# Fewer, wider groups of query tiles in an attention stage, and moved weight scans behind it

## The chip, the cores and the metric

The program runs on one core of a Trainium2 chip. The metric is the device time of one execution in microseconds (us). Engines: PE = TensorE (PEld its weight loads), DVE = VectorE, ACT = ScalarE, POOL = GpSimd, SP = SyncE, whose queue issues the transfers.

## What is computed

A masked attention (4 batches, 8 heads, 576 positions, head size 64) and two feed-forward layers on its 2304 x 512 output:

```python
scores = q @ k.T / 8                       # heads 0-3: keys 0..31 back; heads 4-7: keys with the same index mod 32
x = softmax(where(mask, scores)) @ v       # reshaped to 2304 x 512
x = (h * cos(h)) @ w_out,  h = x @ w_in    # 512 -> 2048 -> 512
y = (silu(x @ w_gate) * (x @ w_val)) @ w_out2   # 512 -> 1536 -> 512
```

The weights arrive as 64-bit floats and are turned into float32 on the chip, then each into two float16 parts (high and low). The factor before the split comes from the largest absolute value of the whole matrix, so a matrix is scanned once before any of it can be split.

## The kernel before

**Attention.** Heads go in pairs; a unit is one pair in one batch, and there are 16 units, local ("l", keys up to 31 back) and strided ("s") in turn. A local unit has 9 tiles of 64 queries against 96 keys, a strided one 11 tiles of 54 queries against 54 keys. `groups` (L78) cuts a unit into groups: 3+3+3 tiles, or 4+4+3, so 48 groups in all, one for each step of the loop over `k` (L818). Groups of an s and an l unit alternate: a round of six steps does two units.

A group passes through the engines over eight steps (`LAGS`, L51). PE: `scores` (fp32 products L470, a filler of bfloat16 ones into the rest of the PSUM bank L472, and the mask added through an identity L473). DVE: `top` (row maximum, L478). One step later ACT: `exps` (one instruction per tile, L484). Two steps later DVE: `sums` (L493, L496), POOL: `norm` (L498). Five steps later PE: `transposes` (L504, L508) into one of two PSUM tiles `tp`, ACT: `evac` to SBUF (L515). Six: PE `values` (L526). Seven: ACT `put` (L539 local, L548 strided) into `xy`. After the last group the pipeline drains, with `keep_warm` (L816) and the first product of slot 0 on PE.

Other work is mixed in from a queue `fill`: `pump` (called in L858) emits entries until their cost passes a share per step, `PUMP` from step `KP` on. For w_in an entry chain converts a tile (ACT L254, DVE L257, L261, L265), and after the last tile, the scale and the split follow: high part on ACT (L275, entry cost 0), low part on DVE (L278, cost 0.7). Behind each low part stood one scan of a w_out tile (L204, cost 0.63). Raw tiles come through a ring of `RAW` = 6 buffers of 512 KB; `RELEASE` is the step from which those of w_out may start.

**First layer.** Its loop counts slots: 5 blocks of tokens times 16 columns tiles of w_in. A slot is one first product on PE (L584 to L586, 12 products of up to 512 columns), then ACT L617, DVE L620, ACT L624, DVE L627, ACT L631, POOL L632. Slot 0 lies in the drain. The first `HEAD` slots have only first products; from then on the queue of finished tiles is shortened to `MINLAG` at `RATE` a slot, each shortening being a second product with a w_out tile (`need(("out", m))`). In the same stretch the w_out tiles are converted and split ("cv", "arena") and w_gate and w_val scanned. `HSHARE`, `SHARE` and `SHARE2` set how much of `fill` a slot takes. The second layer follows once all its weights are rewritten.

Of the kernel before, what the change touches and what calls it, by code (L numbers as in the profile page):

```python
# [10 lines left out]
F32 = mybir.dt.float32  # L11
# [39 lines left out]
LAGS = (2, 5, 6, 7)  # L51
WARM = 11
PUMP, KP = 1.05, 8
XSAT = 12
EARLY, K0 = 1, 1
HEAD, HSHARE = 16, 0.8
RATE, MINLAG = 0.7, 2
ALONE = 4
RAW = 6
RELEASE = 30  # L60
# [3 lines left out]
SHARE, SHARE2, SB = 0.89, 0.82, 2  # L64
# [13 lines left out]
def groups(p):  # L78
    return [(0, 3), (3, 3), (6, 3)] if is_local(p) else [(0, 4), (4, 4), (8, 3)]


def build(tc, qk_l, qk_s, v_l, v_s, w_in, w_out, w_gate, w_val, w_out2, fixed, out):
    nc = tc.nc
    wide = w_in.dtype != F32
    with ExitStack() as ctx:
# [322 lines left out]
        words = [128, 2 * LW, 2 * SW]  # L408
        fix = ap.tile([128, sum(words)], F32, name="fix", bufs=1)
        id32, ml, ms = (fix[:, sum(words[:i]):sum(words[:i + 1])] for i in range(3))  # L410
        ml, ms = (t.bitcast(BF16).rearrange("p (n w) -> p n w", n=4) for t in (ml, ms))
        e_s = [ap.tile([128, 2, 64, 2], F32, name=f"e_s{i}", bufs=1) for i in range(4)]
        e_l = [ap.tile([128, 3, LW + 1], F32, name=f"e_l{i}", bufs=1) for i in range(4)]
# [38 lines left out]
        class Group:  # L452
# [7 lines left out]
            def scores(self):  # L460
# [3 lines left out]
                mask = (ml[:, 0:3] if self.g == 0 else ml[:, 1:4]) if self.loc else ms[:, 0:n]  # L464
# [35 lines left out]
            def transposes(self):  # L500
                if self.loc:
                    self.tp = pa.tile([128, self.n, 128], F32, name="tp")[0:LW]
                    for i in range(self.n):
                        nc.tensor.transpose(self.tp[:, i, :], self.t[:, i, 0:LW], id32)  # L504
                else:
                    self.tp = pa.tile([128, 2, 128], F32, name="tp")
                    for i in range(2):
                        nc.tensor.transpose(self.tp[:, i, :], self.t[:, i].rearrange("p k u -> p (k u)"), id32)  # L508

            def evac(self):  # L510
                if self.loc:
                    self.pt = ap.tile([LW, 3, 128], F32, name="pt", bufs=2)
# [860 lines left out]
```

## Time and profile before

| | us |
|---|---|
| runs | 862.55 median of 3 (862.11 to 862.92) |
| profiled execution | 862.11, span of its instructions 860.2 |
| PE / DVE / ACT / POOL busy | 845.0 / 653.6 / 520.5 / 196.5 |
| attention, to the first product of slot 1 | 102.05 |

The profile draws a matmul with a modelled end, so that its duration includes the run through the array, and neighbours overlap; what a phase takes from PE is read from its start to the next phase's start. ACT and DVE rows overlap in the same way. In the timeline, an fp32 product counts as two instructions.

### The profile page before, as it was taken

Reading aid. Unit: us, or ns where it says so; the run is one execution under the profiler, and the core shown is the slowest. Engines: PE = TensorE matmul, PEld = TensorE weight load, DVE = VectorE, ACT = ScalarE, POOL = GpSimd, SP = SyncE. Lnnn points to the kernel's source line nnn. Section 1 sums busy time; section 2 is a strip of 40 time slices with the busy share of each in tenths; the row PEclk is TensorE's granted clock in tenths of the full one; section 3 lists DMA queues with packets and bytes.
Section 4 is the critical chain, followed back from the end, with each engine's and each line's share of the span. In section 5 each row is a group of like instructions: output and inputs, shape, how many; then the busy total and the mean of one; then the engine's idle time right before and its main releaser. Section 6 shows DMA issues by size and latency. Waiting matters only on the chain.

```text
span 860.2 us, 18371 instructions
## 1 busy us (share of the span) xinstructions
PE 845.0 (98%) x7223; PEld 601.9 (70%) x7223; DVE 653.6 (76%) x1256; ACT 520.5 (61%) x1047; POOL 196.5 (23%) x249
## 2 busy tenths in 40 slices
PE   9999999999999999999999999999999999999998
PEld 5776544444444444555666787888888899999998
DVE  6999989997888978789996378567656755665562
ACT  6898889654657767768885466545344444444440
POOL 4444234211446446422223000000000000000000
PEclk9999999999999999999999999999999999999999
DMA  9998832896567566415356157667776777788894
GB/s 366 408 370 269 278 102 74 288 340 252 164 205 248 190 209 206 174 49 175 118 210 239 73 186 274 219 224 258 231 273 224 257 266 276 291 302 315 320 331 150
DMA packets 53606, 202.23 MB, mean 235 GB/s; under 512 B 5264, under 2 KB 15888, under 8 KB 49680
## 3 DMA queue, kind: packets, MB, share of 16 engines
q1 hardware_dynamic: 53520, 201.06, 66.9%
q8 instruction: 57, 0.93, 0.4%
q14 instruction: 29, 0.24, 0.1%
HBM read 177.05 MB, written 23.99 MB: 234 GB/s over the span
## 4 chain that ended last, share of the span: by engine, by line
PE 82%; DVE 10%; ACT 5%; issue 2%; DMA 1%; POOL 0%; ACTq 0%; DVEq 0%
PE acc L737 14%; PE bank L584 13%; PE bank L586 13%; PE bank L585 13%; PE acc L584 9%; PE acc L586 9%; PE acc L585 9%; DMA raw<-w_in 1%; DVE xs L278 1%; PE bank L470 1%; DVE arena L710 1%; DVE ls L493 1%; DVE arena L1235 1%; DVE tb L620 1%; ACT xy L548 1%
## 5 line engine op out<-in xcount | busy, mean ns | idle before, releaser
L584 PE MATMUL bank<-xs,wi 128*128 128x256 f16 (+3 forms) x776 | 231.1, 298 | 5.2 <-DVE arena L1235 2.3
L586 PE MATMUL bank<-xs,wi 128*128 128x256 f16 (+3 forms) x776 | 231.1, 298 | 0.0
L585 PE MATMUL bank<-xs,wi 128*128 128x256 f16 (+3 forms) x776 | 231.1, 298 | 0.0
L632 POOL TENSOR_TENSOR arena<-tb,arena 128x512 f16<-128x512 f32 (+1 forms) x80 | 91.2, 1141 | 239.1 <-ACT arena L631 223.8
L585 PEld LDWEIGHTS <-wi 128*128 128x128 f16 x880 | 86.1, 98 | 42.7 <-issue 8.6
L584 PE MATMUL acc<-arena 128*128 128x512 f16 (+1 forms) x320 | 114.5, 358 | 0.0
L585 PE MATMUL acc<-arena 128*128 128x512 f16 (+1 forms) x320 | 114.5, 358 | 0.0
L586 PE MATMUL acc<-arena 128*128 128x512 f16 (+1 forms) x320 | 114.5, 358 | 0.0
L584 PEld LDWEIGHTS <-wi 128*128 128x128 f16 x880 | 86.1, 98 | 36.0 <-issue 1.1
L586 PEld LDWEIGHTS <-wi 128*128 128x128 f16 x880 | 86.1, 98 | 34.8
L737 PEld LDWEIGHTS <-arena 128*128 128x128 f16 x1080 | 100.7, 98 | 8.2
L722 POOL TENSOR_TENSOR wi<-tb 128x256 f32<-128x256 f32 (+1 forms) x30 | 20.2, 673 | 340.5 <-DVE tb L704 340.5
L704 DVE SCALAR_TENSOR_TENSOR tb<-tb,c,arena 128x512 f32<-128x512 f32 (+1 forms) x60 | 41.6, 693 | 61.3 <-ACT tb L699 61.3
L707 ACT ACTIVATE arena<-tb 128x256 f16<-128x256 f32 (+3 forms) x59 | 28.9, 489 | 94.3 <-DVE tb L704 90.5
L585 PEld LDWEIGHTS <-arena 128*128 128x128 f16 x600 | 58.7, 98 | 34.1 <-issue 1.4
L737 PE MATMUL acc<-arena 128*128 128x256 f16 (+1 forms) x702 | 82.0, 265 | 0.0
L586 PEld LDWEIGHTS <-arena 128*128 128x128 f16 x600 | 58.7, 98 | 32.9
L584 PEld LDWEIGHTS <-arena 128*128 128x128 f16 x600 | 58.7, 98 | 32.6
L631 ACT ACTIVATE arena<-tb 128x512 f16<-128x512 f32 (+1 forms) x80 | 46.7, 583 | 53.0 <-PE acc L586 51.4
L617 ACT ACTIVATE tb<-bank,quarter,c 128x512 int32<-128x512 f32 (+1 forms) x74 | 53.7, 726 | 34.2 <-PE bank L586 26.4
L1235 DVE TENSOR_TENSOR arena<-bank,cv 128x512 f32<-128x512 f32 (+1 forms) x60 | 38.1, 636 | 45.1 <-PE bank L586 44.1
L699 ACT ACTIVATE tb<-arena,c 128x512 f32<-128x512 f32 (+1 forms) x60 | 40.8, 679 | 40.4 <-DVE arena L1235 39.4
(144 smaller groups left out, 1728.7 us busy)
## 6 DMA issues: line engine op xcount, KB each, us to landing
wi<-w SPq DMA_DIRECT2D x20, 1792.0 KB, 8.1
arena<-w SPq DMA_DIRECT2D x60, 576.0 KB, 4.8
raw<-w_out SPq DMA_DIRECT2D x56, 512.0 KB, 4.7
arena<-w SPq DMA_DIRECT2D x10, 1792.0 KB, 8.9
raw<-w_gate SPq DMA_DIRECT2D x24, 512.0 KB, 4.0
raw<-w_val SPq DMA_DIRECT2D x24, 512.0 KB, 5.7
w<-arena SPq DMA_DIRECT2D x42, 256.0 KB, 3.2
raw<-w_in SPq DMA_DIRECT2D x16, 512.0 KB, 9.1
```

The costliest lines, as they stand in the source:

```text
L584: nc.tensor.matmul(out=o, lhsT=w[:, 0, c], rhs=x[0], start=first, stop=False, **kw)
L585: nc.tensor.matmul(out=o, lhsT=w[:, 0, c], rhs=x[1], start=False, stop=False, **kw)
L586: nc.tensor.matmul(out=o, lhsT=w[:, 1, c], rhs=x[0], start=False, stop=last, **kw)
L617: nc.scalar.activation(out=c["w"].bitcast(I32), in_=c["ph"], func=AF.Identity, scale=turn[c["blk"]], bias=quarter)
L631: nc.scalar.activation(out=g[:, 0, 0:n], in_=w, func=AF.Copy)
L632: nc.gpsimd.tensor_tensor(out=g[:, 1, 0:n], in0=w, in1=g[:, 0, 0:n], op=ALU.subtract)
L699: nc.scalar.activation(out=t, in_=gate, func=AF.Silu, scale=turn_g[c["blk"]])
L704: nc.vector.scalar_tensor_tensor(out=t, in0=t, scalar=s_g[c["blk"]], in1=c["C"][m][:, 1, 0:c["n"]], op0=ALU.mult, op1=ALU.mult)
L707: nc.scalar.activation(out=to, in_=src, func=AF.Copy, scale=2.0 ** -11)
L722: nc.gpsimd.tensor_tensor(out=t_sums[:, 0, 0:h], in0=c["t"][0][:, h:2 * h], in1=c["t"][0][:, 0:h], op=ALU.subtract)
L737: nc.tensor.matmul(out=o[:, c], lhsT=w[:, 256 * i + 128 * c:256 * i + 128 * c + 128], rhs=unit(u)[:, x:x + h], start=j == c == i == 0, sto ...
L1235: nc.vector.tensor_tensor(out=c["C"][m][:, :, h * right:h * right + h], in0=p, in1=t, op=ALU.add)
```

## The change

A unit's tiles go in two groups: 5+4 local, 6+5 strided, so 32 groups and 39 steps instead of 48 and 56, a round being four steps. Fillers and tiles take the new widths; a local group of five is transposed into both `tp` tiles. Three buffers for exponentials instead of four, lags one step shorter. The w_out scans leave the places behind the low parts and stand behind all of them. `PUMP` goes to 1.4 from step 6, the second products start in slot 19 at 1.3 a slot, and the shares of a slot rise slightly. V tiles are loaded at a round's start for that round. Not shown: mask widths, the tile shapes of `mx`, `ls`, `pt`, and the host's layout of the masks.

```diff
--- before.py
+++ after.py
@@ -48,20 +48,21 @@
-LAGS = (2, 5, 6, 7)
+LAGS = (2, 4, 5, 6)
+ROUND = 4
 WARM = 11
-PUMP, KP = 1.05, 8
+PUMP, KP = 1.4, 6
 XSAT = 12
 EARLY, K0 = 1, 1
-HEAD, HSHARE = 16, 0.8
-RATE, MINLAG = 0.7, 2
+HEAD, HSHARE = 19, 0.8
+RATE, MINLAG = 1.3, 2
...
-RELEASE = 30
+RELEASE = 25
...
-SHARE, SHARE2, SB = 0.89, 0.82, 2
+SHARE, SHARE2, SB = 0.92,0.85,2
...
@@ -76,7 +77,7 @@
 def groups(p):
-    return [(0, 3), (3, 3), (6, 3)] if is_local(p) else [(0, 4), (4, 4), (8, 3)]
+    return [(0, 5), (5, 4)] if is_local(p) else [(0, 6), (6, 5)]
@@ -405,12 +406,12 @@
-        e_s = [ap.tile([128, 2, 64, 2], F32, name=f"e_s{i}", bufs=1) for i in range(4)]
-        e_l = [ap.tile([128, 3, LW + 1], F32, name=f"e_l{i}", bufs=1) for i in range(4)]
+        e_s = [ap.tile([128, 3, 64, 2], F32, name=f"e_s{i}", bufs=1) for i in range(3)]
+        e_l = [ap.tile([128, 5, LW + 1], F32, name=f"e_l{i}", bufs=1) for i in range(3)]
...
@@ -469,25 +470,25 @@
-                nc.tensor.matmul(out=b[:, 288:512], lhsT=ones16, rhs=hot[:, 0:224], start=False, stop=False)
+                nc.tensor.matmul(out=b[:, n * w:512], lhsT=ones16, rhs=hot[:, 0:512 - n * w], start=False, stop=False)
                 nc.tensor.matmul(out=self.sc, lhsT=id16, rhs=mask, start=False, stop=True)
...
             def exps(self):
-                self.t = (e_l if self.loc else e_s)[(self.i // 2 * 3 + self.g) % 4]
+                self.t = (e_l if self.loc else e_s)[(self.i // 2 * 2 + self.g) % 3]
...
@@ -498,21 +499,21 @@
             def transposes(self):
-                if self.loc:
-                    self.tp = pa.tile([128, self.n, 128], F32, name="tp")[0:LW]
-                    for i in range(self.n):
-                        nc.tensor.transpose(self.tp[:, i, :], self.t[:, i, 0:LW], id32)
-                else:
-                    self.tp = pa.tile([128, 2, 128], F32, name="tp")
-                    for i in range(2):
-                        nc.tensor.transpose(self.tp[:, i, :], self.t[:, i].rearrange("p k u -> p (k u)"), id32)
+                self.tp = []
+                for a, z in ((0, 3), (3, 5)) if self.loc and self.n > 4 else ((0, self.n if self.loc else 3),):
+                    t = pa.tile([128, 4, 128], F32, name="tp")[0:LW if self.loc else 128, 0:z - a]
+                    self.tp.append((a, z, t))
+                    for i in range(a, z):
+                        nc.tensor.transpose(t[:, i - a, :], self.t[:, i, 0:LW] if self.loc
+                                            else self.t[:, i].rearrange("p k u -> p (k u)"), id32)
             def evac(self):
...
-                nc.scalar.activation(out=self.pt, in_=self.tp, func=AF.Copy)
+                for a, z, t in self.tp:
+                    nc.scalar.activation(out=self.pt[:, a:z], in_=t, func=AF.Copy)
...
@@ -803,22 +804,25 @@
         top_later("in")
-        scan_later("out", 0)
+        later(1.0, lambda: None)
         scale_later(TW_IN, "in")
-        split_chain([("in", j, wi) for j in range(M1)], 2, lambda j: scan_later("out", j + 1) if j + 1 < M1 else top_later("out"))
+        split_chain([("in", j, wi) for j in range(M1)], 2)
+        for j in range(M1):
+            scan_later("out", j)
+        top_later("out")
...
         def keep_warm():
-            t = bank()[:, 0:4 * LW].rearrange("p (n w) -> p n w", w=LW)
+            t = bank()[:, 0:5 * LW].rearrange("p (n w) -> p n w", w=LW)
...
-            i, g = 2 * (k // 6), k % 6
+            i, g = 2 * (k // ROUND), k % ROUND
...
-                if g in (3, 4) and i + g - 1 < len(units):
-                    scale_q(i + g - 1)
+                if g in (1, 2) and i + g + 1 < len(units):
+                    scale_q(i + g + 1)
...
-            if group(0) and g == 5:
-                for j in (i + 2, i + 3):
-                    if i and j < len(units):
+            if g == 0 and i >= 4:
+                for j in (i, i + 1):
+                    if j < len(units):
                         load_v(j)
+            if group(0) and g == ROUND - 1:
                 for j in (i + 6, i + 7):
                     if j < len(units):
                         load_qk(j)
```

**PE in the attention, before** (one s and one l group; `po` is the output of `values`, `fix` holds the mask):

```order
L470 MATMUL bank<-qks 64x54 x8
L472 LDWEIGHTS ones_77
L472 MATMUL bank<-hot,ones_77 128x224
L473 LDWEIGHTS id_76
L473 MATMUL bank<-fix,id_76 128x216
L526 MATMUL po<-pts,v_pair_109 64x54 x8
L508 MATMUL tp<-fix,e_s_99 128x128 x2
L470 MATMUL bank<-qkl 64x96 x6
L472 LDWEIGHTS ones_77
L472 MATMUL bank<-hot,ones_77 128x224
L473 LDWEIGHTS id_76
L473 MATMUL bank<-fix,id_76 128x288
```

**PE there, after:**

```order
L471 MATMUL bank<-qks 64x54 x12
L473 LDWEIGHTS ones_77
L473 MATMUL bank<-hot,ones_77 128x188
L474 LDWEIGHTS id_76
L474 MATMUL bank<-fix,id_76 128x324
L527 MATMUL po<-pt,vl 64x64 x8
L507 MATMUL tp<-fix,e_l_102 96x128 x5
L471 MATMUL bank<-qkl 64x96 x10
L473 LDWEIGHTS ones_77
L473 MATMUL bank<-hot,ones_77 128x32
L474 LDWEIGHTS id_76
L474 MATMUL bank<-fix,id_76 128x480
```

The products of a phase grew from 6 or 8 to 8 to 12, the filler shrank from 224 columns to 188 and 32, and the pieces come in 16 such pairs instead of 24.

**ACT in the drain, before,** up to the last `put` (L539; `wi` is the split of w_in):

```order
L548 ACTIVATE xy_69<-po 128x12x6
L548 ACTIVATE xy_70<-po 128x12x12
L515 ACTIVATE pts<-tp 128x256
L539 ACTIVATE xy_70<-po 128x192
L515 ACTIVATE pt<-tp 96x384
L275 ACTIVATE wi<-wi,s_1656 128x512
L548 ACTIVATE xy_69<-po 128x8x6
L548 ACTIVATE xy_70<-po 128x8x12
L275 ACTIVATE wi<-wi,s_1656 128x512
L539 ACTIVATE xy_70<-po 128x192
```

**ACT there, after** (its lines are one higher):

```order
L516 ACTIVATE pts<-tp 128x384
L276 ACTIVATE wi<-wi,s_1621 128x512 x2
L540 ACTIVATE xy_69<-po 128x192
L540 ACTIVATE xy_70<-po 128x128
L516 ACTIVATE pt<-tp 96x512
L276 ACTIVATE wi<-wi,s_1621 128x512 x2
L549 ACTIVATE xy_69<-po 128x14x6
L549 ACTIVATE xy_70<-po 128x14x12
L276 ACTIVATE wi<-wi,s_1621 128x512 x2
L540 ACTIVATE xy_70<-po 128x256
```

Between the last `exps` and the last `put`, five high parts stood before, and ten stand now, always two in a row.

**DVE in the drain, before:**

```order
L204 TENSOR_REDUCE pw_out<-raw 128x1
L496 RECIPROCAL ls<-ls 128x4
L493 TENSOR_REDUCE ls<-e_l_105 128x3
L151 TENSOR_SCALAR c_1967<-inv_1220,inv_1657 128x1
L278 SCALAR_TENSOR_TENSOR wi<-wi,s_1656 128x512
L496 RECIPROCAL ls<-ls 128x3
L204 TENSOR_REDUCE pw_out<-raw 128x1
L278 SCALAR_TENSOR_TENSOR wi<-wi,s_1656 128x512
```

**DVE there, after:**

```order
L279 SCALAR_TENSOR_TENSOR wi<-wi,s_1621 128x512 x2
L497 RECIPROCAL ls<-ls 128x6
L494 TENSOR_REDUCE ls<-e_l_101 128x4
L152 TENSOR_SCALAR c_1719<-inv_1209,inv_1622 128x1
L279 SCALAR_TENSOR_TENSOR wi<-wi,s_1621 128x512 x2
L497 RECIPROCAL ls<-ls 128x4
L279 SCALAR_TENSOR_TENSOR wi<-wi,s_1621 128x512 x9
L205 TENSOR_REDUCE pw_out<-raw 128x1
L621 SCALAR_TENSOR_TENSOR tb<-bank,c_1719,tb 128x512
L205 TENSOR_REDUCE pw_out<-raw 128x1 x2
```

Beside each low part stood one scan of w_out; now all the low parts come first, and the 16 scans lie between the first layer's own instructions.

## Rows read from the trace of the kernel before

**Rows 1.** The page, busy time of the engines.

```profile
PE 845.0 (98%) x7223; PEld 601.9 (70%) x7223; DVE 653.6 (76%) x1256; ACT 520.5 (61%) x1047; POOL 196.5 (23%) x249
```

**Rows 2.** Windows: busy us of each engine (instructions), granted clock, DMA share, GB/s.

```profile
40.00:50.00 10.00, 10.00 (x169) 7.23 (x168) 9.90 (x26) 9.76 (x40) 5.05 (x8) 1.00 1.03 410
...
180.00:190.00 10.00, 10.00 (x48) 4.51 (x47) 9.93 (x18) 4.63 (x8) 1.16 (x1) 1.00 0.98 361
```

**Rows 3.** Timeline of PE, one s and one l group: start, duration, instruction.

```profile
62.10 0.67 PE L470 MATMUL bank<-qks 64*64 64x54 f32 x16
62.71 0.27 PE L472 MATMUL bank<-hot,ones 128*128 128x224 bf16 x1
62.81 0.26 PE L473 MATMUL bank<-fix,id 128*128 128x216 bf16 x1
63.00 0.68 PE L526 MATMUL po<-pts,v_pair 108*64 108x54 f32 x16
63.61 0.44 PE L508 MATMUL tp<-fix,e_s 128*128 128x128 f32 x2
63.98 0.71 PE L470 MATMUL bank<-qkl 64*64 64x96 f32 x12
64.62 0.27 PE L472 MATMUL bank<-hot,ones 128*128 128x224 bf16 x1
64.73 0.29 PE L473 MATMUL bank<-fix,id 128*128 128x288 bf16 x1
64.94 0.57 PE L526 MATMUL po<-pt,vl 96*64 96x64 f32 x12
65.44 0.53 PE L504 MATMUL tp<-fix,e_l 128*96 128x128 f32 x3
65.91 0.50 PE L470 MATMUL bank<-qks 64*64 64x54 f32 x10
```

**Rows 4.** The same view, an s group of three tiles.

```profile
20.68 0.56 PE L470 MATMUL bank<-qks 64*64 64x54 f32 x12
21.16 0.27 PE L472 MATMUL bank<-hot,ones 128*128 128x224 bf16 x1
21.27 0.23 PE L473 MATMUL bank<-fix,id 128*128 128x162 bf16 x1
21.43 0.56 PE L526 MATMUL po<-pts,v_pair 108*64 108x54 f32 x12
21.92 0.44 PE L508 MATMUL tp<-fix,e_s 128*128 128x128 f32 x2
```

**Rows 5.** Timeline of ACT, from the last scores to the last `put`.

```profile
92.34 0.88 ACT L275 ACTIVATE wi<-wi,s 128x512 f16<-128x512 f32 x1
92.95 0.48 ACT L539 ACTIVATE xy<-po 128x192 f32<-128x192 f32 x1
93.17 0.65 ACT L515 ACTIVATE pt<-tp 96x384 f32<-96x384 f32 x1
93.53 0.96 ACT L484 ACTIVATE e_l<-bank,mx 128x96 f32<-128x96 f32 x3
94.21 0.90 ACT L275 ACTIVATE wi<-wi,s 128x512 f16<-128x512 f32 x1
...
101.65 0.35 ACT L539 ACTIVATE xy<-po 128x192 f32<-128x192 f32 x1
```

**Rows 6.** Timeline of PE: first product of slot 1, and its wait before the second products.

```profile
102.05 0.38 PE L584 MATMUL acc<-xs,wi 128*128 128x512 f16 x1 [0.50 <-ACT xy L539]
...
142.26 0.38 PE L584 MATMUL bank<-xs,wi 128*128 128x512 f16 x1 [1.08 <-DVE tb L627]
```

**Rows 7.** DVE groups by line from 102.1 to 142 us: busy us, mean ns.

```profile
L620 DVE SCALAR_TENSOR_TENSOR tb<-bank,c,tb 128x512 f32<-128x512 f32 x8 | 5.9, 743 | 0.3 <-ACT tb L617 0.3
L627 DVE SCALAR_TENSOR_TENSOR tb<-tb,bank 128x512 f32<-128x512 f32 x7 | 4.7, 678 | 1.0 <-ACT tb L624 1.0
...
L278 DVE SCALAR_TENSOR_TENSOR wi<-wi,s 128x512 f16<-128x512 f32 x5 | 3.7, 744 | 0.0
L204 DVE TENSOR_REDUCE pw_out<-raw 128x1 f32<-128x512 f32 x5 | 3.4, 680 | 0.0
```

More of the change, by code (lines that the diff above doesn't have):

```diff
@@ L407, in build @@
         pa = attn.enter_context(tc.tile_pool(name="pa", bufs=2, space=bass.MemoryType.PSUM))
-        words = [128, 2 * LW, 2 * SW]
+        words = [128, 5 * LW // 2, SW]
         fix = ap.tile([128, sum(words)], F32, name="fix", bufs=1)
         id32, ml, ms = (fix[:, sum(words[:i]):sum(words[:i + 1])] for i in range(3))
-        ml, ms = (t.bitcast(BF16).rearrange("p (n w) -> p n w", n=4) for t in (ml, ms))
-        e_s = [ap.tile([128, 2, 64, 2], F32, name=f"e_s{i}", bufs=1) for i in range(4)]
-        e_l = [ap.tile([128, 3, LW + 1], F32, name=f"e_l{i}", bufs=1) for i in range(4)]
+        ml, ms = (t.bitcast(BF16).rearrange("p (n w) -> p n w", n=n) for t, n in ((ml, 5), (ms, 2)))
+        e_s = [ap.tile([128, 3, 64, 2], F32, name=f"e_s{i}", bufs=1) for i in range(3)]
+        e_l = [ap.tile([128, 5, LW + 1], F32, name=f"e_l{i}", bufs=1) for i in range(3)]
         hot = ap.tile([128, 512], BF16, name="hot", bufs=1)
@@ L463, in scores @@
                 self.sc = b[:, 0:n * w].rearrange("p (n w) -> p n w", w=w)
-                mask = (ml[:, 0:3] if self.g == 0 else ml[:, 1:4]) if self.loc else ms[:, 0:n]
+                mask = ml[:, 1 if self.g else 0:][:, 0:n] if self.loc else ms[:, 0:1].to_broadcast([128, n, w])
                 for i in range(n):
@@ L471, in scores @@
                                          start=i == 0, stop=False)
-                nc.tensor.matmul(out=b[:, 288:512], lhsT=ones16, rhs=hot[:, 0:224], start=False, stop=False)
+                nc.tensor.matmul(out=b[:, n * w:512], lhsT=ones16, rhs=hot[:, 0:512 - n * w], start=False, stop=False)
                 nc.tensor.matmul(out=self.sc, lhsT=id16, rhs=mask, start=False, stop=True)
             def top(self):
-                self.mx = ap.tile([128, 4], F32, name="mx", bufs=3)
+                self.mx = ap.tile([128, 6], F32, name="mx", bufs=3)
                 m = self.mx[:, 0:self.n]
@@ L486, in sums @@
             def sums(self):
-                self.ls = ap.tile([128, 4], F32, name="ls", bufs=5)
+                self.ls = ap.tile([128, 6], F32, name="ls", bufs=5)
                 if self.loc:
-                    self.l, self.e = self.ls[:, 0:3], self.t
+                    self.l, self.e = self.ls[:, 0:self.n], self.t[:, 0:self.n]
                 else:
@@ L777, in quarter_out @@
                 store("12", 0, h)
-        gs = [Group(i + d, g) for i in range(0, len(units), 2) for g in range(3) for d in range(2)]
+        gs = [Group(i + d, g) for i in range(0, len(units), 2) for g in range(2) for d in range(2)]
         load_qk(0)
@@ L1345, in layout @@
     ok = (row + STRIDE - key >= 0) & (row + STRIDE - key < STRIDE)
-    tiles = np.stack([ok & (key >= STRIDE), ok, ok, ok], axis=1)
+    tiles = np.stack([ok & (key >= STRIDE), ok, ok, ok, ok], axis=1)
     mask_l = np.where(np.concatenate([tiles, tiles]), 0.0, MASKED).astype(ml_dtypes.bfloat16)
@@ L1349, in layout @@
     ok = ((row // RJ == key // RJ) & (key % RJ <= row % RJ)) | (row >= SW)
-    tiles = np.stack([ok] * 4, axis=1)
+    tiles = np.stack([ok] * 2, axis=1)
     mask_s = np.where(np.concatenate([tiles, tiles]), 0.0, MASKED).astype(ml_dtypes.bfloat16)
```

4 lines of the change are left out of this document (2 added, 2 removed).

## The prediction

> **What bounds the kernel now.** The page comes first: PE is busy for 845.0 us of 860.2 [rows 1], so a gain must shorten PE's own work or keep it from waiting elsewhere. The windows come next, for the stages that the change touches. In the attention PE is busy all the time at the full granted clock (1.00), but DVE (9.90 of 10 us), ACT (9.76) and the transfers (share 1.03, 410 GB/s) leave almost no room either; at 180 to 190 us, where w_out is converted, DVE is as full (9.93) and the transfers nearly so (0.98) [rows 2]. So the timeline must tell who sets the pace. On PE an s and an l group together go from 62.10 to 65.91, 3.81 us, with no gap, each phase starting where the one before lets it [rows 3]. I take the attention as bound by PE, with little behind it. At its end this turns round: slot 1 starts at 102.05 us, 0.05 after ACT's last put, which begins at 101.65 and lasts 0.35 [rows 5, 6]; there ACT sets the end. After that PE waits once before the second products, 1.08 us, for DVE [rows 6].
>
> **Fewer groups: PE work.** The price of a phase is the distance from its start to the next start. In s groups, scores cost 0.61 us for 16 instructions and 0.48 for 12, values 0.61 and 0.49 [rows 3, 4]: 0.03 an instruction, and 0.09 and 0.13 that come once a phase. The mask's 0.19 for 216 columns, 0.16 for 162 and 0.21 for 288 give 0.0004 a column and 0.095 once. Transposes take 0.37 for two and 0.47 for three: 0.10 each, 0.17 once. A filler of 224 columns takes about 0.11.
>
> A pair of units takes before:
> - s, three groups: scores 1.70, fillers 0.32, masks 0.54, values 1.71, transposes 1.10: 5.37.
> - l, three times 0.64 + 0.11 + 0.21 + 0.50 + 0.47: 5.79. Together 11.16, which is 3.81 + 3.81 + 3.54 for the three pairs of groups [rows 3, 4].
>
> And after, with the same prices:
> - s, 24 and 20 instructions: scores 0.87 + 0.74, values 0.85 + 0.73, masks (324 and 270 columns) 0.23 + 0.205, fillers (188 and 242) 0.09 + 0.11, transposes, three and three, 0.94: 4.77.
> - l, 20 and 16 instructions: scores 1.01 + 0.82, values 0.75 + 0.63, masks (480 and 384) 0.29 + 0.25, fillers (32 and 128) 0.05 + 0.06, transposes, five and four, 0.67 + 0.57: 5.10. Together 9.87.
>
> That is 1.29 us less for each of 8 pairs: **-10.3 us**. Bounds: the once-a-phase part of l phases is no row, only carried over from s, so up to -11. If nothing came once a phase, only filler columns would go: 48 x 224 - 8 x 590 = 6,032 columns at 0.11/224 us, -3.0. I take -10.3, because the s rows show the fixed part in four phases.
>
> Here a rule of the Trainium skill speaks against the change. TensorE: Matmul & The Clock Gate, section "Wait — 56ns, not 53.3ns?", gives a stream of matmuls N/2.4 ns plus about 2.5 ns each, with no price for a change of phase. By it the term would be near the -3.0, and the sum would lie 7.3 us higher; the 216 mask columns above take 0.19 us where it gives 0.09, so the trace speaks for a price.
>
> **Can the others keep this pace?** Per pair of units DVE loses two reductions' and two reciprocals' overhead and nearly all of the w_out scans that stood in the split's steps; it gets a higher `PUMP`: 4 x 1.4 = 5.6 of cost in 9.87 us, against 6.3 in 11.16, which is the same rate. ACT gets the same exponentials. At 9.76 of 10 us it must now do them in 88% of the time, relieved only by some evacuations and puts. The transfers must carry, in a pair of units, 2.2 MB of q, k and v (the tiles' sizes) and 5.6/1.62 = 3.5 raw tiles of 0.52 MB: 4.0 MB in 9.87 us, 409 GB/s, where the busy window gives 410 [rows 2]. POOL's scaling of the fourth pair's q stands early in the third round, and the first 10 MB, which lie ahead of it in the queue, take 25 us; norms wait behind it. And a local group of five takes both `tp` buffers, so that its second tile and the s group after it need the evacuation of the step just before, where before it was one step older. Nothing is priced in a row; bounds are 0 and the 6 us at which half the gain is gone. I take **+2.5**, nearer to nothing, since PE kept its 3.81 with DVE and ACT as full as now.
>
> **The drain.** The splits now come with 2 x 1.4/0.7 = 4 high parts for two steps, against about 1.6 before (1.05/1.33 each), and most of them fall after the last scores. By the order, ten stand between ACT's last exps and last put, where five stood. One takes 0.61 us (92.34 to 92.95, and 94.21 to 94.82); put 0.22, evacuation 0.36, three exps 0.68 [rows 5]. All other ACT work there is nearly the same, and slot 1 waits for the last put. So 5 x 0.61 = **+3.1**. Bounds: 0, if PE had work of its own until then, which its 0.50 of waiting on that put denies [rows 6]; and 8 x 0.61 = 4.9, with the pairs of high parts in the steps before the drain that PE outruns as well. The high parts left behind the last put wait on nothing that PE needs before some slots.
>
> **The scans behind the attention, and slot 19.** The 16 scans of 0.68 us are 10.9 us of DVE. They land in slots 1 to 16, each of which is 2.59 us of PE (12 products of 0.216), while DVE's own share is 0.74 + 0.68 = 1.42 [rows 7]. Between slot 1 and the first second product DVE gets 10.9 us of scans and 3 x 1.42 for three more slots, and loses the five low parts and five scans that before lay there (3.7 + 3.4 [rows 7]): +8.1 us. PE gets 3 x 2.59 = 7.8 more. So the wait of 1.08 [rows 6] stays about as it is, with 0.3 more. The higher rate then asks for 2.3 w_out tiles a slot instead of 1.7, but the sixteenth second product has as many first products before it as today within one, so the same DVE work and transfers have to be done by the same point of PE's work. I take **+0.5**; bounds -1.1 (no wait at all) and +4 (DVE and transfers, at 9.93 and 0.98 [rows 2], fall behind the bursts). The slot shares cost nothing themselves: by the order, no weight step is left in the last slots of the layer, before or after.
>
> **Sum:** -10.3 + 2.5 + 3.1 + 0.5 = -4.2 on the profiled execution's 862.1, so 857.9. That execution lies 0.4 below the median of the three runs, and so the forecast is **858.3 us**.
>
> **Rivals.**
> - *The whole gain stays.* PE's drain has spare products, and the neighbours keep up: the sum without most of the 2.5 and half of the 3.1, 852 to 855. For it: PE's strict 3.81 [rows 3]. Against: the wait on the put [rows 6].
> - *The gain is eaten in the attention.* Either a phase has hardly a fixed price (-3.0 + 3.1 and the waits), or ACT and the transfers, not PE, set the pace at about 10.6 us a pair of units: 8 x 0.56 = -4.5, +3.1, +0.5: 861 to 864, no change within what can be measured. For it: 9.76 and 1.03 [rows 2]. By the page's rule above the result would lie here too.
> - *Slower: w_out comes late.* With the scans after the attention, the scale of w_out exists only some 16 slots on, and 16 conversions with 24 scans of w_gate and w_val must be ready at 2.3 a slot. If DVE cannot use its gaps in the slots, PE waits for the 8.1 us of DVE work at the second products, with only the 4.7 net of the other terms to set against it: 866. It decides as soon as the wait there goes over 4.7. Against: 1.17 us of each slot are free on DVE by rows 7.
> - *The change doesn't do what it says:* ruled out by the order, in which all scans stand behind the last low part and the groups are 32.
>
> **Chances.** Forecast, 855 to 861: 0.57. Whole gain: 0.13. Eaten: 0.20. Slower: 0.10. A measurement of this kernel can tell about 0.2%, 1.7 us, from no change. Below 860.8 lie the whole gain and the forecast but for its upper edge: 0.70. Within 1.7 us: that edge and most of the eaten gain, 0.18. Above 864.3: 0.12. The range reaches from 854.0 (all waits at nothing, -10.3 + 1.8) to 863.5 (the lower end of the eaten case), which leaves out about 2 in 10.
>
> **What would show it.** In the new profile the period of four groups (two pairs) near 60 us should be close to 9.9 us; a steady 10.6 or more with waits for ACT, `tp` or loads says that another engine took over. Slot 1 should start near 97.5 us, with PE ending its wait at an ACT put, and the drain some 3 us longer than now. Before the second products PE should wait 1 to 2 us for DVE; 5 or more there is the slower rival. The granted clock must stay at 1.00 although less filler runs; if it falls anywhere, the prediction is wrong for a reason that is not in the sum. From about 350 us on, both profiles should look the same, shifted.

## The result, and the profile after

The changed kernel takes **871.28 us** (median of 4 runs, 870.72 to 871.89), the kernel before 862.63 beside it: a ratio of **1.0106, 95% interval 1.0093 to 1.0119**. It is slower, 13 us above the forecast and 7.8 above the range.

| start, us | before | after | forecast |
|---|---|---|---|
| first product of slot 0, in the drain | 93.4 | 91.9 | |
| first product of slot 1 | 102.05 | 102.90 | 97.5 |
| first product of slot 17 | 144.8 | 146.1 | |
| first second product (set for slot 16, then 19) | 147.4 | 159.2 | |
| end of the span | 860.2 | 868.9 | |

So nothing is left of the attention's gain when slot 1 starts (+0.85), and from there to the second products' steady run another 7.9 us are lost. From 280 us on both profiles run alike, some 9 us apart. The page of the changed kernel, and what PE waits for from 10 to 300 us (waited for by whom, for whom, us, times, longest):

```profile
PE 839.2 (97%) x7190; PEld 598.8 (69%) x7190; DVE 642.5 (74%) x1208; ACT 518.0 (60%) x1019; POOL 196.5 (23%) x230
```

```profile
PE tp L507 <- POOL e_l L499: 6.7, 10, 1.9
PE acc L587 <- DVE arena L279: 3.7, 3, 2.7
PE tp L507 <- POOL e_s L499: 2.5, 5, 1.0
PE bank L585 <- DVE tb L628: 2.3, 1, 2.3
PE acc L585 <- ACT xy L540: 1.9, 1, 1.9
```

PE's busy time fell by 5.8 us [rows 1], so the work did shrink, and waits that the kernel before did not have took more than that: 9.2 us at the transposes for POOL's norm and 3.7 for the low parts of w_out. Two waits of before have grown: 2.3 instead of 1.1 us for the first layer's own DVE work, 1.9 instead of 0.5 for the put ahead of slot 1. The windows, to be held against [rows 2]:

```profile
40.00:50.00 10.00, 8.96 (x167) 6.76 (x164) 8.85 (x22) 9.27 (x34) 4.58 (x6) 1.00 1.03 409
...
80.00:90.00 10.00, 8.33 (x155) 6.30 (x154) 7.49 (x24) 8.68 (x30) 2.28 (x3) 1.00 0.62 221
90.00:100.00 10.00, 7.52 (x96) 4.79 (x98) 7.00 (x13) 8.99 (x23) 3.03 (x3) 1.00 0.01 2
100.00:110.00 10.00, 8.12 (x44) 3.43 (x43) 8.02 (x12) 6.69 (x12) 0.00 (x0) 0.83 0.30 93
...
180.00:190.00 10.00, 8.71 (x41) 3.67 (x39) 7.51 (x15) 2.69 (x4) 0.00 (x0) 1.00 0.98 351
190.00:200.00 10.00, 8.59 (x32) 3.58 (x33) 9.93 (x18) 6.07 (x10) 1.16 (x1) 0.83 0.96 346
```

Three things stand there. In the attention neither PE nor DVE is full any more. At 90 to 100 us the transfers stand still. And the granted clock is below 1.00 twice, at 100 to 110 and at 190 to 200 us, each time behind a wait of PE. The timeline of one step in the attention shows the first:

```profile
65.27 0.55 DVE L479 TENSOR_REDUCE mx<-bank 128x4 f32<-128x384 f32 x1
...
66.19 0.69 DVE L266 SCALAR_TENSOR_TENSOR wi<-raw,wi 128x512 int32<-128x512 int32 x1
...
66.26 0.91 PE L471 MATMUL bank<-qks 64*64 64x54 f32 x24
...
66.79 0.75 DVE L279 SCALAR_TENSOR_TENSOR xs<-xy,s,xs 128x512 f16<-128x512 f32 x1
...
67.46 0.18 DVE L497 RECIPROCAL ls<-ls 128x5 f32<-128x5 f32 x1
67.55 0.46 DVE L494 TENSOR_REDUCE ls<-e_s 128x6 f32<-128x330 f32 x1
67.81 0.99 POOL L499 TENSOR_TENSOR e_l<-e_l,ls 128x480 f32<-128x480 f32 x1 [2.08 <-DVE ls L497]
67.93 0.49 DVE L479 TENSOR_REDUCE mx<-bank 128x6 f32<-128x324 f32 x1
68.33 1.68 DVE L279 SCALAR_TENSOR_TENSOR xs<-xy,s,xs 128x512 f16<-128x512 f32 x2
...
68.85 0.75 PE L507 MATMUL tp<-fix,e_l 128*96 128x128 f32 x5 [0.75 <-POOL e_l L499]
```

The reciprocal of a group stands on DVE behind the maximum (L479) and the pumped work (L266, L279) of its step, POOL's norm behind the reciprocal, the transposes behind the norm, and on PE the next scores behind those transposes. DVE's maximum waits for those scores. That is a loop; by the order, with lags of 2 and 4 it closes over two steps, with 2 and 5 over three. And after the drain, PE at the lower level of the clock, 1.2 GHz (the 12 products of slot 1 take 4.27 us, from 102.90 to 107.17, and not 2.59):

```profile
102.90 0.50 PE L585 MATMUL acc<-xs,wi 128*128 128x512 f16 x1 [1.88 <-ACT xy L540]
103.19 0.63 PE L586 MATMUL acc<-xs,wi 128*128 128x512 f16 x1
...
107.17 0.38 PE L585 MATMUL bank<-xs,wi 128*128 128x512 f16 x1
```

### The profile page after: what moved, and what is told of

Same layout as the page of the kernel before. It is cut to its first block, busy times and chain, and to the rows that moved or that the text cites. A ratio compares the mean times of both kernels' runs of the same rounds, so it can differ in the third digit from the quotient of the medians.

```text
span 868.9 us, 18107 instructions
## 1 busy us (share of the span) xinstructions
PE 839.2 (97%) x7190; PEld 598.8 (69%) x7190; DVE 642.5 (74%) x1208; ACT 518.0 (60%) x1019; POOL 196.5 (23%) x230
## 4 chain that ended last, share of the span: by engine, by line
PE 80%; DVE 10%; DMA 5%; ACT 3%; issue 1%; POOL 1%; SPq 0%; POOLq 0%; ACTq 0%; DVEq 0%
PE acc L738 14%; PE bank L585 13%; PE bank L587 13%; PE bank L586 13%; PE acc L587 8%; PE acc L585 8%; PE acc L586 8%; DMA raw<-w_in 2%; DMA raw<-w_gate 2%; DVE xs L279 1%; DMA v_pair<-v_s 1%; PE bank L471 1%; PE tp L507 1%; DVE pw_in L258 1%; DMA fix<-fixed 1%
## 5 line engine op out<-in xcount | busy, mean ns | idle before, releaser
L632 ACT ACTIVATE arena<-tb 128x512 f16<-128x512 f32 (+1 forms) x80 | 46.6, 583 | 54.1 <-PE acc L587 50.4
```

Source lines behind the costliest of these rows:

```text
L632: nc.scalar.activation(out=g[:, 0, 0:n], in_=w, func=AF.Copy)
```

## Experiments

Ratios are to the kernel before, with 95% intervals; a time is the median of a version's runs, and its trace is that of one of them. "The period" is the distance on PE between the scores of one round and the next (the phase of 24 instructions, L471): 11.15 us before, 10.91 in the changed kernel (22.86 to 77.43, five rounds).

### One part of the change undone at a time

**norm_early**

```diff
                 group(LAGS[0]).sums()
+                group(LAGS[0]).norm()
...
             pump(PUMP if k >= KP else 0)
-            if group(LAGS[0]):
-                group(LAGS[0]).norm()
```

> Theory (a loop sets the pace): in the changed kernel the scores of one step must pass DVE's maximum, the pumped weight work of that step, the reciprocal and POOL's norm before the transposes two steps on may run, and those stand ahead of PE's next scores. Putting reciprocal and norm directly behind the sums takes the maximum and the pumped work out of that loop. PE's waits on POOL's norm (9.2 us in the changed kernel) fall below 3, the period of four groups goes from 10.75 us to 9.9 to 10.2, slot 1 starts at 97 to 99 instead of 102.9, and the time is 865 to 868. Rival (DVE, ACT or the transfers are simply full): the period stays at 10.6 or more, PE waits for something else instead, 870 to 872.

877.19 us, 1.0159 (1.0121 to 1.0197), slower than the changed kernel (runs from 872.13, the one profiled, to 879.59); period 11.2, slot 1 at 106.4. The order opens the loop, but PE's waits on the norm only fell from 9.2 to 7.7 us, so this run does not show what the loop costs. It had a price that neither theory had: DVE became full (48.97 of 50 us from 22 to 72, against 45.59), with the same instructions. DVE groups from 10 to 90 us (busy us, mean ns), the changed kernel and then this one:

```profile
L266 DVE SCALAR_TENSOR_TENSOR wi<-raw,wi 128x512 int32<-128x512 int32 x16 | 12.3, 768 | 0.4
L258 DVE TENSOR_REDUCE pw_in<-raw 128x1 f32<-128x512 f32 x16 | 10.8, 675 | 0.0
L262 DVE TENSOR_SCALAR wi<-wi 128x512 int32<-128x512 int32 x16 | 8.0, 499 | 0.2 <-ACT wi L255 0.2
```

```profile
L266 DVE SCALAR_TENSOR_TENSOR wi<-raw,wi 128x512 int32<-128x512 int32 x16 | 14.2, 886 | 0.4
L262 DVE TENSOR_SCALAR wi<-wi 128x512 int32<-128x512 int32 x16 | 12.0, 750 | 0.2 <-ACT wi L255 0.2
L258 DVE TENSOR_REDUCE pw_in<-raw 128x1 f32<-128x512 f32 x16 | 10.8, 676 | 0.0
```

And in its timeline, the same DVE operation without and with POOL at work:

```profile
24.82 0.42 DVE L262 TENSOR_SCALAR wi<-wi 128x512 int32<-128x512 int32 x1
...
32.35 0.99 POOL L499 TENSOR_TENSOR e_l<-e_l,ls 128x480 f32<-128x480 f32 x1 [1.03 <-ACT pts L516]
...
32.53 1.10 DVE L262 TENSOR_SCALAR wi<-wi 128x512 int32<-128x512 int32 x1
```

The conversion ended 0.3 us after POOL was done (33.34): beside it, it made little headway. The reduction (L258) is as fast as before. With the norm behind the pumped work, as both kernels have it, POOL works mostly beside the sums and the maximum, which are reductions too. The Trainium skill, Trainium Architecture — The Big Picture, section "What this means for kernel authors", says that DVE and GpSimd share a port pair as an exclusive lock; the conversion's rows agree.

**lag_five**

```diff
-LAGS = (2, 4, 5, 6)
+LAGS = (2, 5, 6, 7)
```

> Transposes one step later (lags 2, 5, 6, 7 as in the kernel before), the rest as changed. Theory of the loop: the loop closes over three steps instead of two, so the waits on POOL's norm fall below 2 us and the period is 9.9 to 10.1; one more step in the drain costs up to 1 us; slot 1 at 98 to 100, 866 to 869. Rival (engines or transfers full): period 10.6 or more, slot 1 at 103 or later, 871 to 873.

870.81 us, 1.0095 (1.0070 to 1.0120): no gain that can be told. Yet the loop was the cause in the attention: the waits on POOL's norm fall from 9.2 to 1.7 us, the period to 10.21, and slot 0's first product comes at 83.1 instead of 91.9. Then the drain takes 15.7 us, not 11.0, and slot 1 starts at 98.8. Its last steps on ACT:

```profile
95.55 1.35 ACT L276 ACTIVATE wi<-wi,s 128x512 f16<-128x512 f32 x2
...
96.78 0.61 ACT L549 ACTIVATE xy<-po 128x84 f32<-128x84 f32 x2
97.16 1.33 ACT L276 ACTIVATE wi<-wi,s 128x512 f16<-128x512 f32 x2
...
98.40 0.36 ACT L540 ACTIVATE xy<-po 128x256 f32<-128x256 f32 x1
```

Two high parts stand before each evacuation or put, so a step of the drain takes ACT 1.6 to 2.2 us, and there is one step more. The lead of 4.1 us at slot 1 is not lost at the second products: slot 50 of the first layer starts at 351.6, 5.3 us ahead of the changed kernel. One wait of 3.0 us near 365 us, with a granted clock of 0.69 from 368 to 372 behind it, then takes 4.0 of that.

**second_from_16**

```diff
-HEAD, HSHARE = 19, 0.8
-RATE, MINLAG = 1.3, 2
+HEAD, HSHARE = 16, 0.8
+RATE, MINLAG = 0.7, 2
```

> Second products from slot 16 at 0.7 a slot, as in the kernel before; the rest as changed. Theory (w_out is late because its scans were moved): w_out's parts are ready at the same times whatever PE asks for, so the waits move but don't go: over 6 us of waiting at the first second products, and the first layer ends within 2 us of the changed kernel's 470 us mark; 869 to 876. Rival (slot 19 and 1.3 a slot ask for bursts): the waits of 6 us between 140 and 220 us fall under 2 and the clock stays at 1.00 there; 863 to 866.

870.03 us, 1.0086 (1.0064 to 1.0107). Nearly as the theory had it: the low parts of w_out come when they come, and the waits move (4.9 us on w_out's parts, where over 6 were expected).

**scans_beside**

```diff
-RELEASE = 25
+RELEASE = 21
...
-        later(1.0, lambda: None)
+        scan_later("out", 0)
         scale_later(TW_IN, "in")
-        split_chain([("in", j, wi) for j in range(M1)], 2)
-        for j in range(M1):
-            scan_later("out", j)
-        top_later("out")
+        split_chain([("in", j, wi) for j in range(M1)], 2, lambda j: scan_later("out", j + 1) if j + 1 < M1 else top_later("out"))
```

> The w_out scans stand beside the low parts of w_in again (and w_out's loads are released four steps earlier, 21 for 25, so that they are there); the rest as changed. Theory (w_out late by its scans): the conversions of w_out start some 8 us earlier, PE's waits at the second products and the low clock at 190 to 200 us go, the attention keeps its period of 10.7: 862 to 866. Rival (rate and slot 19 are what hurts): waits on w_out's low parts stay at 4 us or more: 869 to 872.

873.78 us, 1.0121 (1.0088 to 1.0154): slower than both theories had it. The first conversion of w_out comes at 146.6, hardly before the 149.8 of the changed kernel. Slot 50 starts 2.6 us ahead of the changed kernel, and the wait near 365 us takes more than that again. A sum that I had not made goes with the late conversion: the attention pumps 33 steps x 1.4 = 46.2 of cost where the kernel before pumps 48 x 1.05 = 50.4. At slot 1 the kernel before has 11 low parts and 12 scans behind it, this one 8 and 8. Among the versions with the scans beside the low parts, the first conversion follows the pumped cost: 146.6 us here, 136.9 in drain_light (47.4 of cost), 123.4 in the kernel before, 110.7 in groups_only (53.6).

### Two groups with everything else as before, and parts of the change put into it

**groups_only**

```diff
-LAGS = (2, 4, 5, 6)
+LAGS = (2, 5, 6, 7)
...
-PUMP, KP = 1.4, 6
+PUMP, KP = 1.575, 6
...
-HEAD, HSHARE = 19, 0.8
-RATE, MINLAG = 1.3, 2
+HEAD, HSHARE = 16, 0.8
+RATE, MINLAG = 0.7, 2
...
-RELEASE = 25
+RELEASE = 20
...
-SHARE, SHARE2, SB = 0.92,0.85,2
+SHARE, SHARE2, SB = 0.89,0.82,2
```

and the scans' places as in scans_beside. Not everything is as before: 34 steps x 1.575 pump 53.6 of cost, 3.2 more than the kernel before.

> Two groups a unit alone: transposes one step later again, scans of w_out beside the low parts (released at step 20), second products from slot 16 at 0.7, the shares of the kernel before, and a pump of 1.575 a step from step 6, so that four steps carry 6.3 of cost like six steps before. Theory (the weight work on DVE is what sets the first 220 us; the changed kernel pumps 33 x 1.4 = 46.2 of it in the attention where the kernel before pumps 48 x 1.05 = 50.4, and lets DVE idle in the loop): DVE stays over 9.6 of 10 in the attention, the period is 9.9 to 10.3, slot 1 starts at 97 to 100, the first conversion of w_out ends before 130 us, and the time is 856 to 861. Rival (wider groups bring nothing, since DVE or ACT cannot do their share in less time): period 10.7 or more, 862 to 867.

**860.82 us, 0.9987 (0.9978 to 0.9996)**: the best version of this study with all its work, ahead of both kernels, but by less than 0.2% of the one before. Where PE does not wait, a round takes 9.77 us:

```profile
44.91 0.91 PE L471 MATMUL bank<-qks 64*64 64x54 f32 x24
...
54.68 0.91 PE L471 MATMUL bank<-qks 64*64 64x54 f32 x24
...
64.46 0.91 PE L471 MATMUL bank<-qks 64*64 64x54 f32 x24
```

But with its waits the mean of five rounds (20.56 to 76.23) is 11.13 us, and slot 1 starts at 102.2; both were expected lower. One loss on the way: ACT, in order, waits for a raw tile that the transfers have not brought, PE for ACT's evacuation, and then the clock falls to 1.2 GHz.

```profile
35.32 0.67 ACT L255 ACTIVATE wi<-raw 128x512 f32<-128x512 f32 x1 [1.82 <-DMA raw<-w_in]
...
36.85 0.60 PE L507 MATMUL tp<-fix,e_l 128*96 128x128 f32 x2 [1.68 <-ACT pts L516]
```

```profile
36.00:38.00 2.00, 1.15 (x14) 0.81 (x16) 1.97 (x5) 1.97 (x9) 1.39 (x2) 0.74 1.01 404
38.00:40.00 2.00, 2.00 (x32) 1.49 (x30) 1.80 (x5) 1.00 (x4) 1.14 (x2) 0.50 1.02 411
```

Another is the drain, 13.1 us from slot 0's first product; a third is PE's wait of 1.8 us for w_in's maximum (scale_gap, below).

**groups_lag4**

```diff
-LAGS = (2, 5, 6, 7)
+LAGS = (2, 4, 5, 6)
```

> groups_only with the changed kernel's lags 2, 4, 5, 6. Theory (loop of scores, maximum, pumped work, norm, transposes closed over two steps): PE's waits on POOL's norm go from 1.2 to 9 us or more, the period of four groups from 10 to 10.8 or more, slot 1 starts at 107 to 110, 866 to 872. Rival (the loop is covered by the drain or by the transfers): waits on the norm without a later slot 1, 860 to 863.

868.33 us, 1.0075 (1.0062 to 1.0088), 7.5 us above groups_only; slot 0's first product comes 7.7 us later, slot 1 at 106.0. The period, 11.19 (25.15 to 81.11), is hardly above groups_only's mean, so the 7.7 us lie mostly in the rounds before and behind these five. The waits are back, 11.2 us instead of 1.2:

```profile
PE tp L507 <- POOL e_l L499: 9.8, 14, 1.9
PE tp L507 <- POOL e_s L499: 1.4, 5, 0.5
```

At slot 50 it is 4.1 us behind groups_only; the rest of the 7.5 is the wait near 365 us.

**groups_behind**: the groups_only with the scans, and the empty entry, where the change has them.

> groups_only with the w_out scans behind all low parts, as the change has them. Theory (without a scan of 0.68 us on DVE beside each low part, ACT with its high parts is the slower engine of the pair and DVE idles; the scans then come on top in the slots, and the transfers stand still until they begin): slot 1 2 to 4 us later, DVE under 8 of 10 between 80 and 100 us, the conversions of w_out 8 us or more later, 865 to 868. Rival (the place of the scans does nothing by itself): 860 to 862.

876.45 us (873.66 in the profiled run), 1.0158 (1.0144 to 1.0172), 15.6 us above groups_only, more than I expected, and the conversions come 12 us later. DVE sinks to 7.06, and the ring of six raw tiles shows why the transfers stand still: it fills with w_out tiles whose scans come only after the last low part. Windows, and the wait that follows on PE:

```profile
90.00:100.00 10.00, 6.70 (x61) 3.77 (x60) 7.06 (x13) 8.61 (x22) 2.95 (x3) 0.84 0.00 0
110.00:120.00 10.00, 4.95 (x23) 2.06 (x21) 7.61 (x12) 3.20 (x5) 0.45 (x1) 0.87 1.03 413
```

```profile
121.06 0.29 PE L145 MATMUL bank<-tops,ones 128*128 128x128 bf16 x1 [6.11 <-DVE tops L139]
```

The matmul that spreads w_out's maximum stands between products of the slots. PE, in order, waits there until the ten scans that had no tile yet are done, one each 1.28 us.

**groups_second19**

```diff
-HEAD, HSHARE = 16, 0.8
-RATE, MINLAG = 0.7, 2
+HEAD, HSHARE = 19, 0.8
+RATE, MINLAG = 1.3, 2
```

> groups_only with the second products from slot 19 at 1.3 a slot. Theory (what hurt there in the changed kernel was that w_out's parts came late, not when PE asked for them): no wait over 1 us on w_out's low parts, 859.5 to 862.5. Rival (slot 19 and 1.3 ask for bursts that the transfers at 0.95 cannot feed): waits of 3 us or more at 170 to 220 us, 864 to 867.

866.01 us, 1.0040 (1.0027 to 1.0053), 5.2 us above groups_only. Both theories missed. The waits on low parts stay at 0.7 us and at 345 us the two run level; the loss is one wait, 220 us later, where the reader of another scale is late, and the low clock (0.70 from 364 to 368) behind it:

```profile
365.11 0.32 PE L585 MATMUL bank<-xs,wi 128*128 128x384 f16 x1 [2.72 <-DVE q L146]
```

**drain_light**

```diff
-            pump(PUMP if k >= KP else 0)
+            pump(0 if k < KP else PUMP if k < len(gs) else DRAIN)
...
+DRAIN = 0.8
```

> groups_only with one edit: after the last scores a step pumps 0.8 instead of 1.575. Theory (the drain is bound by ACT, whose high parts of w_in stand between the exponentials, evacuations and puts that PE waits for): the drain from the first product of slot 0 to slot 1 goes from 13.1 to 9 or 10 us, slot 1 starts at 97 to 99 instead of 102.2, w_out's first conversions come later but still before 135, and the time is 856 to 859. Rival (the drain's own chain of exponentials, norms and puts is as long): slot 1 after 101, 860 to 863.

864.53 us, 1.0024 (1.0013 to 1.0035). The pumped work does set the drain, though less than expected: 11.1 us instead of 13.1, slot 1 at 99.8. That ACT's part of it sets it is what groups_free, below, speaks for. But the weight work left out there is missing later: the first conversion is at 136.9 instead of 110.7, and at slot 17 PE is 1.7 us behind groups_only. The gain went into a later wait and came out larger.

**pump_ramp** and **scale_gap**: an entry of cost 1.0 between w_in's top and its scale (both), and the pump that follows the transfers (pump_ramp).

```diff
         top_later("in")
+        later(1.0, lambda: None)
...
-            pump(PUMP if k >= KP else 0)
+            pump(0 if k < 7 else 1.45 if k < 18 else 1.7 if k < len(gs) else 1.575)
```

> groups_only with a pump that follows the transfers (from step 7: 1.45 a step to step 17, 1.7 to step 31, 1.575 in the drain) and an empty entry of cost 1.0 between the top of w_in and its scale. Theory (what is left of groups_only's attention gain is lost where ACT, in order, waits for raw tiles that the full transfers have not brought, 4.2 us between 24 and 50 us, and where PE waits 1.8 us for the top of w_in; the low clock behind the first of them costs as much again): ACT's waits on raw fall under 1.5 us, the clock stays at 1.00 until 80 us, slot 1 at 97 to 100, 856 to 859. Rival (ACT and DVE are full there, so that the work only moves): slot 1 at 101 or later, 860 to 863.

> groups_only with the empty entry of cost 1.0 alone. Theory: PE's wait of 1.8 us for the top of w_in goes, all else stays: slot 1 1 to 2 us earlier, 859 to 861. Rival (it only moves to the next wait): no change within 1 us of 860.8, slot 1 at 102.

pump_ramp: 865.39 us, 1.0039 (1.0025 to 1.0053). ACT's waits for raw tiles fell from 4.2 to 1.76 us, but another spreading matmul, that of block 0's scale, now came too early:

```profile
58.58 0.27 PE L145 MATMUL bank<-tops,ones 128*128 128x128 bf16 x1 [3.00 <-DVE tops L139]
```

```profile
60.00:64.00 4.00, 4.00 (x51) 3.06 (x51) 2.22 (x7) 2.82 (x10) 1.28 (x2) 0.50 1.00 399
```

scale_gap: 863.35 us (861.75 in the profiled run), 1.0011 (1.0002 to 1.0020), above both theories. Slot 1 at 99.6 and still 2.0 us ahead of groups_only at 346 us; the wait near 365 us took all of it.

### Weight work by itself

**scans_behind**: the kernel before with the scans moved, as the change has it, and with the change's empty entry of cost 1.0.

> The kernel before with one part of the change: the w_out scans stand behind all low parts. The cost pumped in the attention is the same, so by the theory of the backlog w_out's conversions begin as early as before within 5 us, and all that comes is a longer drain, since ACT gets the high parts of w_in closer together: slot 1 1 to 3 us later, 863 to 866. Rival (the scans' place alone makes w_out late): conversions 8 us or more later than before, 3 us or more of waiting on w_out's low parts, 867 to 872.

867.92 us, 1.0067 (1.0054 to 1.0081). The rival was nearer: slot 1 2.1 us later as I had it, but the first conversion at 133.8 instead of 123.4. The same cost was pumped; its order (low parts without a scan between them, the ring of raw tiles full, the empty entry) lost 5.8 us. The empty entry by itself is scale_gap, where the first conversion stays at 111.0.

**pump_full**

```diff
-PUMP, KP = 1.4, 6
+PUMP, KP = 1.6, 5
```

> The changed kernel with a pump of 1.6 from step 5: 34 x 1.6 = 54.4 of cost in the attention, more than the 50.4 of before. Theory (loop plus backlog): the added work stands inside the loop of scores, maximum, pumped work, norm and transposes, so the period grows to 11 or more and slot 1 comes at 105 to 107, but w_out's conversions begin 8 us or more earlier than the 150 of the changed kernel and the waits at the second products fall to half: 867 to 871. Rival (slot 19 and the rate of 1.3 make the waits): they stay at 6 us or more, 873 to 876.

880.89 us, 1.0219 (1.0205 to 1.0233), beyond both ranges. The conversions begin at 122.9, as the sum of pumped cost says, but slot 1 is at 107.9, and w_out's spreading matmul stops PE for 4.3 us. More weight work in a loop that is already the bound makes the attention later.

**no_scans** and **after_free**: the changed kernel without DVE's 16 scans of w_out; in no_scans their entries cost 0, in after_free they keep their cost and so every place in the order.

> The changed kernel without the 16 scans of w_out on DVE (its scale comes from a constant; the tiles are still loaded and freed, and the entries cost nothing): 10.9 us of DVE less, the transfers as they are. Theory (DVE's backlog of weight work sets when w_out is ready): slot 1 stays near 103, the first conversion of w_out ends near 125 to 135 instead of 150, the waits at the second products and the low clock at 190 to 200 us go: 859 to 864. Rival (transfers at 0.95 and more, or the rate of 1.3, set it): the waits at 180 to 220 us stay, 867 to 871.

> The changed kernel without the same 16 scans, entries and order kept; there they stand between 104 and 143 us, in the slots. Theory (weight work comes late and is paced by its places in the order of the slots, and by the transfers, not by DVE's speed there): DVE has room in those slots already, so at most 2 us are gained: 869 to 872. Rival (DVE's load in the slots makes w_out late): waits at 140 to 160 us go and 4 us or more are gained: 863 to 867.

871.29 us, 1.0108 (1.0094 to 1.0122), and 873.90 us, 1.0137 (1.0120 to 1.0153). Neither gains at the end. In no_scans the wait on low parts does fall from 3.7 to 0.6 us, but slot 1 comes at 107.4 behind a clock of 0.66 from 90 to 100 us; slot 50 starts 3.6 us ahead of the changed kernel, and the meeting near 365 us takes that back. The pair tells one thing apart, the first conversion of w_out (no_scans, then after_free):

```profile
112.11 0.69 DVE L267 SCALAR_TENSOR_TENSOR cv<-raw,cv 128x512 int32<-128x512 int32 x1
```

```profile
151.75 0.68 DVE L268 SCALAR_TENSOR_TENSOR cv<-raw,cv 128x512 int32<-128x512 int32 x1
```

Both take the same 10.9 us from DVE. Only the one whose entries cost nothing starts earlier: when w_out comes is set by the places that the costs give it among the slots, not by DVE's speed.

**groups_free** and **before_free**: groups_only and the kernel before without the same scans, order kept.

> groups_only without DVE's 16 scans of w_out (the scale comes from a constant; entries, their cost, the order of all other instructions and the transfers stay): 10.9 us less for DVE between 75 and 106 us. Theory (with PE's phases shortened, DVE is the engine that sets the pace up to the second products, so PE's saved 9 us come out as waits): the drain shortens, slot 1 starts at 97 to 100 instead of 102.2, and 3 us or more of it last to the end: 854 to 858. Rival (ACT with its high parts, and the transfers, set it): slot 1 within 1 us of 102, 860 to 862.

> The kernel before without the same 16 scans, nothing else. Theory: there PE sets the pace and waits little, so that DVE's 10.9 us bring 0 to 1.5 us: 860.7 to 862.5. Rival (DVE sets the pace there too): 857 to 860.

860.32 us, 0.9981 (0.9972 to 0.9990), and 861.18 us, 0.9990 (0.9980 to 0.9999): 0.5 and 0.8 us for 10.9 us of DVE. My theory that DVE's load takes the gain fell here. The windows of groups_free say who does, in the drain:

```profile
80.00:90.00 10.00, 9.04 (x142) 6.33 (x142) 5.99 (x14) 10.00 (x37) 2.76 (x4) 1.00 0.98 370
90.00:100.00 10.00, 7.01 (x100) 4.55 (x101) 5.75 (x12) 8.79 (x23) 1.89 (x2) 1.00 1.02 410
```

DVE is at 6 of 10, ACT at 10.00 and 8.79, as in groups_only, and the drain stays at 13.1 us (87.17 to 100.22). Slot 1 starts 2.0 us earlier, more than the rival had, less than my theory.

**second_from_22**

```diff
-HEAD, HSHARE = 19, 0.8
+HEAD, HSHARE = 22, 0.8
```

> The changed kernel with the second products from slot 22 instead of 19, still 1.3 a slot. Theory (w_out's low parts come at their own times, about 159 to 218 us, and PE waits only because it asks too early): the waits on w_out's low parts fall from 3.7 us to under 1.5 and the clock at 190 to 200 us stays up: 864 to 868. Rival (the weight work is paced by the slots, so later second products only make it later): waits as before or more, 870 to 874.

875.19 us, 1.0148 (1.0130 to 1.0166). The waits on low parts stay (3.8 us), since the conversions move along with the slots: the second tile is converted at 165.3 instead of 157.7. PE does not ask too early; the weight work is paced by the slots, and comes late.

## Why the prediction was wrong

Two terms failed. In the sum's own terms the forecast was -10.3 + 2.5 + 3.1 + 0.5; the profiled executions give about -11.0 + 9.5 + 2.3 + 7.9 = +8.7 us.

**PE's phases: right.** The forecast said 9.87 us for a pair of units; where PE does not wait, groups_only has 9.77 against 11.15, or -11.0 if all eight pairs went so, where -10.3 was taken. The Trainium skill's rule that I weighed (TensorE: Matmul & The Clock Gate, section "Wait — 56ns, not 53.3ns?"), by which only -3.0 would come, was not borne out: a change of phase has its price.

**Others' keeping pace, "+2.5": the step that failed first.** Slot 0's first product came 1.5 us earlier, so of 11.0 us 9.5 went. I named ACT, the transfers, POOL's scaling of q and the `tp` tiles, and, but for `tp`, looked at throughput only. What bound was a latency: the lag from 5 to 4, which the section on the change lists and no term of mine priced. lag_five (waits 9.2 to under 2 us, slot 0's first product 8.8 us earlier) and groups_lag4 (7.7 us later than in groups_only) show it. Where a step later is given back, the next limits stand close: raw tiles at 1.02 of the transfers, and ACT.

**The drain, "+3.1": right mechanism, size near.** 11.0 us against 8.7, +2.3, with slot 1 behind an ACT put, as said. What I did not see is that ACT's work is a floor there: when PE gets there earlier the drain lengthens (15.7 us in lag_five, with one step more), so an earlier end of the scores does not reach slot 1 in full.

**Scans and slot 19, "+0.5": wrong by 7.4,** the two falls of the clock included. I set the same DVE work against the same PE work and concluded that nothing changes. Three things were left out. The attention pumps 46.2 of cost instead of 50.4, although its rate per us is the same, as I wrote. A scan beside each low part keeps DVE busy while ACT makes the next high part, and keeps the ring of raw tiles turning; without it the transfers stand still at 90 to 100 us (0.01). And DVE cannot "use its gaps": its order is fixed, and the entries' costs give each scan its slot. That is shown by scans_behind (+5.8 in the kernel before) and by no_scans against after_free; how the 7.4 us divide among the three was not measured.

**The clock.** "If it falls anywhere, the prediction is wrong for a reason that is not in the sum": it fell twice, behind PE's waits. Slot 1 alone paid 4.27 - 2.59 = 1.7 us, the fall at 192 us by its length about as much.

**The rivals.** The slower one had the place and the mechanism, w_out late, and 0.10. Its condition, that DVE cannot use its gaps, was the true case; its price, 866, was low, since it counted the attention's gain as there. "Eaten in the attention" came true as well, by another mechanism than its two. I had them as exclusive; both happened.

**What does not add up at the end.** Undone alone in the changed kernel, the lag, the second products and the scans bring -0.5, -1.2 and +2.5 us; put alone into groups_only they cost 7.5, 5.2 and 15.6. One place accounts for much of this, the meeting near 365 us, which lies in slots 50 to 60 (profiled executions):

| us | slot 50 starts | slots 50 to 60 take |
|---|---|---|
| changed kernel | 356.9 | 41.8 |
| lag_five | 351.6 | 45.8 |
| second_from_16 | 354.5 | 41.8 |
| scans_beside | 354.3 | 45.8 |
| groups_only | 347.9 | 41.7 |
| groups_lag4 | 352.0 | 46.0 |
| groups_second19 | 347.4 | 46.7 |
| groups_behind | 357.8 | 43.9 |

Up to slot 50 the lag is worth 5.3 us in the changed kernel and 4.1 in groups_only, nearly the same; the second products 2.4 and -0.5; the scans 2.6 and 9.8. Then a wait of some 3 us, in most of them with a fall of the clock behind it, costs 2 to 5 us in some orders and next to nothing in others. Why was not followed up, so it stays open whether a retuned order would keep more than groups_only does.

## What to carry over

Before a stage of a software pipeline is brought a step nearer, follow the loop through every in-order engine, with the filler work that stands in it, and set it against the number of steps over which it closes: a full engine in the windows says nothing of that. In a schedule whose filler is placed by costs, count the total placed ahead of each point where PE needs it (steps x share), not the rate. And a gain on the busiest engine is worth what the next meeting with the other engines lets through: compare versions ahead of such a meeting as well as at the end.

## What the runs showed of the hardware

A wait of 1 to 3 us on PE is often followed by some 3 to 10 us at 1.2 GHz, but not always: behind the same wait of 2.7 us near 365 us the clock fell in groups_second19 and stayed at 1.00 in scale_gap. Nor is it always in the same place: the changed kernel and second_from_16 have the same order up to slot 12, but at 90 to 100 us the one keeps a granted clock of 1.00, and the other has 0.83 and starts slot 1 at 104.9 instead of 102.9:

```profile
90.00:100.00 10.00, 7.92 (x77) 4.84 (x77) 6.07 (x12) 7.47 (x20) 3.02 (x3) 0.83 0.00 0
```

And DVE's conversion of a tile, 0.42 us alone, took 1.10 beside POOL's norm (rows of norm_early); its reduction of the same tile did not change (676 ns against 675).
